# First batch's attention with four buffers of each kind, held loads, and a second warming product

## The chip, the cores and the metric

The program runs on one core of a Trainium2 chip. The metric is device time in microseconds (us), the median of several runs. PE is the matmul engine, ACT and DVE the two engines that work on vectors, POOL a fourth, slower one, and SP the engine that only issues DMAs.

## The reference

Multi-scale attention over 4 batches, 8 heads, 576 positions and 64 dimensions, then two feed-forward layers on 2304 tokens of width 512, all in float32:

```python
q_d, k_d, v_d = means over groups of 4 positions      # 144 pooled positions
out_up = np.repeat(sm_attn(q_d, k_d, v_d), 4, axis=2)
mask = np.abs(pos[:, None] - pos[None, :]) < 4        # a band of 7 positions
out_local = softmax(where(mask, q @ k.T / 8, -1e9)) @ v
x = (out_up + out_local) as (2304, 512)
x = (sigmoid(x @ w_gate) * (x @ w_val)) @ w_out       # d_ff 1536, "layer 1"
h = x @ w_in                                          # d_ff 2048, "layer 2"
out = (h * sigmoid(1.702 * h)) @ w_out2
```

## The kernel before

**Matmuls.** A float32 product is three PE products of reduced precision: `passes` (L939 to L941) multiplies hi x hi, hi x lo, lo x hi, where `parts_of` (L876, L879) has split each operand (`whi`, `wlo`, `xhi`, `xlo`, `ghi`, `glo`): ACT rounds the high part, DVE or POOL subtracts. Layer 1 is worked through by `visit`, batch by batch: for each of 12 hidden blocks `f`, `hidden` makes gate (part 0) and value (part 1) in a `ph` bank, four groups of three products each, and one block later `result` adds part 2 into four `acc` banks. Weights of layer 1 come from memory as 64-bit words, 512 KB for each part, and `convert` makes 32-bit ones: two passes on ACT (L865, L867) and one on DVE (L869). Four staging buffers `w64` take the loads; the 36 converted parts stay in the "weight places" `wr` and `w` for the later batches.

**Attention.** A `Job` is one batch `b` and one pair of heads `hp`, four for a batch. In order: `load` (qT, kT), `pools` (means over 4 on POOL, L638 and L640), `scores` (96 small matmuls, L674), softmax on DVE and ACT, `down` (pooled scores, L724, and `pooled_softmax`), `down_t` (transposes, L784), `values` (bands of v, L799, pooled values, L821, `up`, the sum `xf`, then `xhi` and `xlo`). v is pooled by PE with a matrix `ones` for batch 0 (`pool_tiles`, L592). The buffers of a kind are two (`sc` and `pdt` one), so a pair waits for an earlier one; only q and k of batch 0 have four, two of them in weight places not yet used (`qt0`, `kt0`). Batches 1 to 3 are "merged": pooled scores are made with the scores, half of the bands with the transposes; batch 1 also has its mask added by PE instead of DVE (L668, `masked`). Batch b's attention runs beside layer 1 of batch b - 1; batch 0's runs alone.

**What sets the order.** Every instruction is an `op` with an engine, an estimate of its time, the buffers it reads and writes, a due time and an earliest time. `Plan.order` walks a model of the five engines and always takes the ready `op` with the earliest due time; this fixes each engine's queue when the program is built, and on the chip each engine only follows its queue and waits for the others. Due times come from `T0` (layer 1 begins), `EARLY`, `FIRST`, `Job.t0` and `Job.t1`. Where PE's model has a gap, `order` fills it with "warming" products of zeros (L1433), at least one before each `op` other than the large products; they stop at the first product into `acc`. All DMAs are issued by SP, in the order of its queue.

Of the kernel before, what the change touches and what calls it, by code (L numbers as in the profile page):

```python
# [79 lines left out]
class Plan:  # L80
# [14 lines left out]
    WARM_LEAST = 1  # L95
    BEGIN = {"pe": 0.0, "act": 2000.0, "dve": 2200.0, "pool": 3900.0, "sp": 600.0}
# [47 lines left out]
    def order(self):  # L144
# [34 lines left out]
        while count:  # L179
# [109 lines left out]
def tile_multiscale_attention_gated_ffn(  # L289
# [83 lines left out]
    wslots = [Slot(x[:, i]) for x in low + top for i in range(2)]  # L373
    for f in range(NF1):
        for part in range(3):
            plan.ring(f"w{f}_{part}", [wslots[2 * NF1 + f if part == 2 else 2 * f + part]])
# [9 lines left out]
    first = [x.rearrange("p a b -> p (a b)").bitcast(F32) for x in top[-4:]]  # L386
    firsts = [Slot(x[:, :n]) for x, n in zip(first, (S + 8, KPAD + S + 5) * 2)]
    plan.ring("qt0", firsts[::2])
    plan.ring("kt0", firsts[1::2])
    for n, x in enumerate(wslots[-8:]):  # L390
        x.under = (firsts[n // 2],)
# [8 lines left out]
    qslots, kslots, vslots, pslots = (plan.rings[nm][0] for nm in ("qt", "kt", "vt", "pt"))  # L400
# [70 lines left out]
    for s in [*qslots, *plan.rings["qt0"][0]]:  # L471
        nc.vector.memset(s.t[:, S:], 0.0)
    for s in [*kslots, *plan.rings["kt0"][0]]:
        nc.vector.memset(s.t[:, :KPAD], 0.0)
        nc.vector.memset(s.t[:, KPAD + S:], 0.0)
# [44 lines left out]
    EARLY = 16.0e3  # L520
    AHEAD = 15.0e3
    FIRST = ((-14.0e3, 14.0e3), (-13.0e3, 16.0e3), (-12.0e3, 18.0e3))
# [19 lines left out]
    class Values:  # L542
# [6 lines left out]
        def load(self):  # L549
            b, c = self.b, slice(self.c0, self.c0 + VC)  # L550
            if b:
                self.vt, self.vd, self.vg = buf("vt"), buf("vd"), buf("vg")

            hp = self.job.hp
            d, after = (self.job.t0 - 3000.0, self.job.t0 - 12000.0) if b else (4500.0 * hp, 4500.0 * hp)
            for kh in range(2) if b else ():
                dma(self.vg.t[:, kh], v[b, kh * 4 * GH:(kh + 1) * 4 * GH, c].rearrange("(g r) d -> g r d", r=4),
                    GH * 4 * VC * 4, [], [(self.vg, kh)], d, after)
            d, after = (self.job.due(0.2), self.job.t0 - 9000.0) if b else (4000.0 * hp, 4000.0 * hp)
            if not b:  # L560

                if hp:
                    return
                c, n, t, d, after = slice(0, DM), 2, vboth.rearrange("p g h c -> p g (h c)"), -19.2e3, 3.5e3
                bs = [self.vt, halves[0, 1].vt]
            else:
                n, t, bs = 1, self.vt.t, [self.vt]
            for i in (0, 2, 1, 3):
# [5 lines left out]
                dma(t[32 * i:32 * i + 32, g0:g1], src, 32 * (g1 - g0) * n * VC * 4, [], [(x, i) for x in bs],  # L574
                    d, after)
            dma(t[3:NU + 1, 0], v[b, :NU - 2, c], (NU - 2) * n * VC * 4, [], [(x, 4) for x in bs], d, after)
            row = NQ * (NT - 1) - 3
            dma(t[96:96 + S - row, NG - 1], v[b, row:S, c], (S - row) * n * VC * 4, [], [(x, 5) for x in bs],
                d, after)

        def pool_tiles(self):
# [3 lines left out]
            at = self.job.due(0.55)  # L585
# [22 lines left out]
    class Job:  # L608


        def __init__(self, b, hp):
            self.b, self.hp = b, hp
            if b == 0:
                a, z = -EARLY, T0 - EARLY
            else:
                a, z = visits[b - 1]["t"] - LEAD, visits[b]["t"] - (SLACK if b < B - 1 else SLACK7)
            step = (z - a) / NHP
            self.t0, self.t1 = a + hp * step, a + (hp + 1.6) * step
            self.banks = twos if b == 0 else twos[:1]
            self.merged = b > 0 and (b, hp) != (1, 0)  # L620
# [3 lines left out]

        def load(self):
            b, hp = self.b, self.hp
            early = b == 0 and hp > 1
            self.qt, self.kt = (buf("qt0"), buf("kt0")) if early else (buf("qt"), buf("kt"))
            d, after = self.t0 - 4000.0, self.t0 - 13000.0
            if b == 0:  # L630
                d, after = -20.0e3 + 500.0 * hp, (0.0, 0.0, 9.5e3, 12.0e3)[hp]
            dma(self.qt.t[:, :S], qT[b, hp], P * S * 4, [], [self.qt], d, after)
            dma(self.kt.t[:, KPAD:KPAD + S], kT[b, hp], P * S * 4, [], [self.kt], d, after)

        def pool4(self, dst, src, bsrc, due):
            half = buf("half")
# [13 lines left out]
        def pools(self):  # L650
            for nm in ("qd", "kd", "sc", "nm", "sm", "pd", "nmd", "smd", "pt", "tt"):
                setattr(self, nm, buf(nm))
# [5 lines left out]
        def scores(self):  # L658
# [5 lines left out]
            masked = self.b == 1  # L664
# [15 lines left out]
            if not self.merged:  # L680
                op("pe", 1500.0 + 200.0 * masked, scored, [qt, kt, *[identb][:masked]], [ss, sc], when)
# [56 lines left out]
        def pooled_softmax(self, ss, c, at, masked):  # L738

            nmd, smd, pd = self.nmd, self.smd, self.pd  # L740
            op("dve", dve_ns(4 * G), lambda: nc.vector.reduce_max(
                nmd.t.rearrange("p (h r) -> p h r", h=2),
                ss.t[:GH, :, c:c + 2 * G].rearrange("p h (r k) -> p h r k", k=G), axis=AX.X),
               [ss, *masked], [nmd], at)
            op("act", 200.0, lambda: nc.scalar.mul(nmd.t, nmd.t, -SCALE_D), [], [nmd], at)
# [10 lines left out]
            def inv():  # L756
                nc.vector.tensor_scalar_add(smd.t, smd.t, 1.0e-9)
                nc.vector.reciprocal(smd.t, smd.t)

            op("dve", 305.0, inv, [], [smd], at)  # L760
# [8 lines left out]
        def down_t(self):  # L769
            self.pdt = buf("pdt")  # L770
# [32 lines left out]
        def values(self):  # L803
# [21 lines left out]
            xf = buf("xf")  # L825
# [28 lines left out]

    def convert(src, out, due, at=None, after=None):

        w = buf("w64")
        if at is None:
            at, after = due - 5000.0, due - AHEAD
        op("sp", P * 4096, lambda: nc.sync.dma_start(out=w.t, in_=src), [], [w], at, after)  # L860

        def words(n, dtype=I32):
# [3 lines left out]
            out.t.bitcast(F32), words(1, F32), AF.Prelu, scale=2.0 ** -112, alpha=-2.0 ** 32), [w], [out], due)  # L866
        op("act", act_ns(DM), lambda: nc.scalar.activation(  # L867
# [88 lines left out]
    def hidden(vi, f, t):  # L956
# [3 lines left out]
        xh, xl = xs[layer, j]  # L960
        hb = []
        th = buf("th")
        for part in range(2 if layer == 1 else 1):
            h = bank(hs_) if layer == 1 else fixed(f % 4)
            w = weights(vi, f, part, t)
            for k in range(NK):
# [3 lines left out]
                   w[0] + [(b, k) for b in (xh, xl)], [h] if part else [h, th], t))  # L970
# [407 lines left out]
    def make_ones():  # L1378
        nc.gpsimd.memset(ones.t, 0.0)
        for i in range(4):  # L1380
            c = 30 + 36 * (i % 2)
            part = ones.t[32 * i:32 * i + 32, c:c + 6]
            nc.gpsimd.memset(part, 1.0)
            nc.gpsimd.affine_select(out=part, in_=part, pattern=[[-4, 6]], compare_op=ALU.is_ge,
                                    fill=0.0, base=-3, channel_multiplier=1)
            nc.gpsimd.affine_select(out=part, in_=part, pattern=[[4, 6]], compare_op=ALU.is_ge,
                                    fill=0.0, base=6, channel_multiplier=-1)

    op("pool", 1500.0, make_ones, [], [ones], -4.0e3)
# [9 lines left out]
    halves[0, 0].load()  # L1399
# [79 lines left out]
```

## Time and profile before

| | us |
|---|---|
| runs | 922.09, 919.75, 920.48 |
| median | 920.48 |
| profiled execution | 919.47 |
| its span | 917.8 |
| PE busy | 907.8 (99%) |
| DVE, ACT, POOL busy | 691.3, 544.0, 80.5 |
| chain that ended last | 98% PE |

The span goes from the first to the last instruction of the profiled execution. A busy PE says little by itself, since warming products count too and the ends of pipelined matmuls are modelled: what a stretch is worth is read from the start times of its matmuls. Everything of attention of batch 0 lies in the first 61 us.

### The profile page before, as it was taken

To read this page: it belongs to the slowest core of one execution; us is meant where nothing else is said; L and a number is where in the kernel's file an instruction comes from. 1 tells how busy PE (TensorE), PEld (TensorE's weight loads), DVE (VectorE), ACT (ScalarE), POOL (GpSimd) and SP (SyncE) were. 2 spreads that over 40 slices of the span, in tenths; PEclk is the share of its full clock that TensorE was granted. 3 is DMA by queue.
4 is the path that set the end of the run, shared out by engine and by line. 5 is a ranking of instruction groups with operands and counts; after the bars stand their busy time and mean duration, and the time that the engine had idled before them with its cause. 6 is when DMAs were issued, how large, how long until landed. Compare 5 with 4: busy or idle time off the path is not lost.

```text
span 917.8 us, 18930 instructions
## 1 busy us (share of the span) xinstructions
PE 907.8 (99%) x7392; PEld 761.9 (83%) x7392; DVE 691.3 (75%) x1291; ACT 544.0 (59%) x1163; POOL 80.5 (9%) x124
## 2 busy tenths in 40 slices
PE   8999999999999999999999999999999999999998
PEld 4678888888888887889999998888888988888886
DVE  4777776776576766799999898878976779877742
ACT  4788885656666666665545655545665655535541
POOL 6221100111011100010000000000301001000000
PEclk9999999999999999999999999999999999999999
DMA  9559672574365734434311751002531002000431
GB/s 286 139 193 261 197 216 57 164 213 148 126 190 181 237 116 145 153 109 141 108 51 41 223 196 46 37 33 73 193 125 70 1 1 69 35 35 35 167 98 47
DMA packets 63949, 113.76 MB, mean 124 GB/s; under 512 B 8241, under 2 KB 29563, under 8 KB 63858
## 3 DMA queue, kind: packets, MB, share of 16 engines
q1 hardware_dynamic: 63858, 112.54, 38.7%
q8 instruction: 58, 0.95, 0.4%
q14 instruction: 33, 0.27, 0.1%
HBM read 82.37 MB, written 30.15 MB: 123 GB/s over the span
## 4 chain that ended last, share of the span: by engine, by line
PE 98%; POOL 1%; issue 0%; DVE 0%; POOLq 0%
PE ph L939 14%; PE ph L940 13%; PE ph L941 13%; PE acc L939 9%; PE acc L941 8%; PE acc L940 8%; PE pa L940 7%; PE pa L939 7%; PE pa L941 7%; PE pa L799 2%; PE pa L674 1%; PE pa L724 1%; PE acc L1433 1%; PE pa L821 1%; PE pa L784 1%; PE acc L799 1%
## 5 line engine op out<-in xcount | busy, mean ns | idle before, releaser
L939 PE MATMUL ph<-xhi,whi 128*128 128x512 f32 (+1 forms) x344 | 135.1, 393 | 0.0
L940 PE MATMUL ph<-xhi,wlo 128*128 128x512 f32 (+1 forms) x344 | 131.6, 383 | 0.0
L941 PE MATMUL ph<-xlo,whi 128*128 128x512 f32 (+1 forms) x344 | 131.5, 382 | 0.0
L876 ACT CAST whi<-w 128x512 fp32r<-128x512 f32 x140 | 85.5, 612 | 59.9 <-PE ph L941 33.2
L879 DVE TENSOR_TENSOR wlo<-w,whi 128x512 fp32r<-128x512 f32 x137 | 95.4, 698 | 29.7 <-ACT whi L876 29.3
L879 DVE TENSOR_TENSOR wlo<-wr,whi 128x512 fp32r<-128x512 f32 x106 | 69.8, 660 | 41.2 <-ACT whi L876 39.9
L939 PEld LDWEIGHTS ph<-xhi,whi 128*128 128x128 f32 x344 | 64.7, 188 | 15.2 <-issue 2.1
L941 PEld LDWEIGHTS ph<-xlo,whi 128*128 128x128 f32 x344 | 64.8, 188 | 12.9
L876 ACT CAST whi<-wr 128x512 fp32r<-128x512 f32 x106 | 60.2, 570 | 25.2 <-PE acc L941 12.2
L940 PEld LDWEIGHTS ph<-xhi,wlo 128*128 128x128 f32 x344 | 64.9, 189 | 11.7
L939 PE MATMUL acc<-ghi,whi 128*128 128x512 f32 (+1 forms) x192 | 73.7, 384 | 0.0
L941 PE MATMUL acc<-glo,whi 128*128 128x512 f32 (+1 forms) x192 | 72.3, 377 | 0.5 <-DVE glo L879 0.5
L1053 DVE TENSOR_TENSOR w<-pa,w 128x512 f32<-128x512 f32 (+1 forms) x112 | 70.4, 629 | 2.4 <-PE pa L941 1.9
L940 PE MATMUL acc<-ghi,wlo 128*128 128x512 f32 (+1 forms) x192 | 72.2, 376 | 0.0
L876 ACT CAST w<-w 128x512 fp32r<-128x512 f32 x62 | 37.9, 619 | 43.1 <-PE acc L940 23.6
L940 PE MATMUL pa<-w,wlo 128*128 128x512 f32 (+1 forms) x166 | 60.6, 365 | 0.0
L941 PE MATMUL pa<-w,whi 128*128 128x512 f32 (+1 forms) x166 | 60.6, 365 | 0.0
L939 PE MATMUL pa<-w,whi 128*128 128x512 f32 (+1 forms) x166 | 60.6, 365 | 0.0
L879 DVE TENSOR_TENSOR w<-w,w 128x512 fp32r<-128x512 f32 x58 | 41.2, 716 | 19.0 <-ACT w L876 18.9
L973 ACT ACTIVATE th<-ph 128x512 f32<-128x512 f32 (+1 forms) x44 | 24.6, 559 | 39.2 <-PE ph L941 39.0
L978 DVE SCALAR_TENSOR_TENSOR th<-th,ph 128x512 f32<-128x512 f32 (+1 forms) x44 | 28.1, 638 | 24.5 <-PE ph L941 19.6
L867 ACT ACTIVATE w<-w 128x512 int32<-128x512 uint32 x68 | 45.2, 670 | 0.0
(281 smaller groups left out, 2222.5 us busy)
## 6 DMA issues: line engine op xcount, KB each, us to landing
w<-w SPq DMA_DIRECT2D x68, 512.0 KB
w2d<-we SPq DMA_DIRECT2D x32, 256.0 KB
w<-gd SPq DMA_DIRECT2D x32, 256.0 KB
gd<-w SPq DMA_DIRECT2D x30, 256.0 KB
st<-x2d SPq DMA_DIRECT2D x52, 128.0 KB
w<-w2d SPq DMA_DIRECT2D x16, 256.0 KB
wr<-w2d SPq DMA_DIRECT2D x16, 256.0 KB
qt<-qT SPq DMA_DIRECT2D x14, 288.0 KB
```

The source lines that it names most:

```text
L674: nc.tensor.matmul(ss.t[32 * i:32 * i + 32, h, g * NU:(g + 1) * NU], qt.t[hs, NQ * t:NQ * t + 32], kt.t[hs, NQ * t:NQ * t + NU], start=not ...
L724: nc.tensor.matmul(ss.t[:GH, h, c + r * G:c + (r + 1) * G], qd.t[h * D:(h + 1) * D, r * GH:(r + 1) * GH], kd.t[h * D:(h + 1) * D, :], star ...
L799: nc.tensor.matmul(ss.t[h * D:(h + 1) * D, s, q:q + NQ], vt.t[ks, g, v0 + h * D:v0 + (h + 1) * D], tt.t[ks, h, g, :NQ], start=True, stop=T ...
L867: op("act", act_ns(DM), lambda: nc.scalar.activation(words(0), words(0, U32), AF.Copy, scale=2.0 ** -29 * (1.0 - 2.0 ** -12), bias=2.0 ** ...
L876: op("act", act_ns(n), lambda: nc.scalar.copy(vh(), vm()), [rm], [rh], due)
L879: return lambda: on.tensor_sub(vl(), vm(), vh().bitcast(F32))
L939: nc.tensor.matmul(o, lhi, rhi, start=first, stop=False, skip_group_check=more)
L940: nc.tensor.matmul(o, llo, rhi, start=False, stop=False, skip_group_check=more)
L941: nc.tensor.matmul(o, lhi, rlo, start=False, stop=last, skip_group_check=more)
L973: op("act", act_ns(n, True), lambda h=h: nc.scalar.activation(th.t[:, :n], h.t[:, :n], AF.Tanh, scale=0.5 if layer == 1 else 1.702 / 4.0), ...
L978: op("dve", dve_ns(n), lambda: nc.vector.scalar_tensor_tensor(th.t[:, :n], th.t[:, :n], 1.0, hb[-1].t[:, :n], op0=ALU.add, op1=ALU.mult), ...
L1053: op("dve", dve_ns(N), lambda: nc.vector.tensor_add(tmp.t[:, o, :N], b.t[:, :N], tmp.t[:, i, :N]), [b, (tmp, i)], [(tmp, o)], t)
```

## The change

For batch 0, attention gets more room: places of weights that are not needed yet hold two further `qt`, `kt`, `pt`, `tt`, `xf`, three further `sc` and up to three of `pd`, `pdt` and the small ones, and the order in which weights take the places is changed so that these are taken last. All pairs of batch 0 but the first become merged, and all have the mask from PE. The loads of q, k and v of batch 0 go through `dma_in_turn`: each one waits on SP until all older ones have landed but the last 0.9 MB; v goes ahead of the fourth pair instead of the third. No other DMA is planned before 17 us. Layer 1 is planned from 30 us instead of 37 (`T0`), the pairs of batch 0 start 3 us apart. For some pairs of batch 0 the means over 4, the scaling of the pooled weights and other steps move between POOL, ACT and DVE; `ones` is made on DVE. Of every three conversions one does the shift on DVE instead of ACT. From 25 us of the plan on at least two warming products stand before each small `op`, not one.

```diff
+    WARM_MORE = 25.0e3
-                                n = max(n, self.WARM_LEAST)
+                                n = max(n, self.WARM_LEAST + (t >= self.WARM_MORE))
...
+    over = [*low[-3:], *top[-6:]]
+    for n, x in enumerate(over):
+        if n < 3:
+            a, b_, c = parts_in(x, NS, 4 * G, 8 * NG)
+            some = [("sc", Slot(tiled(a))), ("pdt" if n == 2 else "pd", Slot(squares(b_)))]
...
+        elif n < 5:
+            some = [("xf", Slot(parts_in(x, S)[0]))]
+        else:
+            a, b_ = parts_in(x, NQK, NP)
+            some = [(("qt", "kt")[n % 2], Slot(a)), (("tt", "pt")[n % 2], Slot(tiled(b_)))]
...
+    for nm, some in early.items():
+        plan.ring(nm + "0", plan.rings[nm][0] + some)
...
-        op("sp", nbytes, lambda: nc.sync.dma_start(out=out_, in_=in_), reads, writes, due, after)
+        op("sp", nbytes, lambda: nc.sync.dma_start(out=out_, in_=in_), reads, writes, due, max(after, FREE))
+    FREE = 17.0e3
+    DEEP = 900.0e3
+    def dma_in_turn(out_, in_, nbytes, writes):
...
+        while behind and ahead + started[behind - 1][0] <= DEEP:
+            behind -= 1
+            ahead += started[behind][0]
+        def fn():
+            x = nc.sync.dma_start(out=out_, in_=in_).ins
+            started[n].append(x)
+            if behind:
+                tc.add_manual_dep(x, started[behind - 1][2].name, mybir.DependencyInfo(
+                    mybir.DependencyClass.Sync, mybir.DependencyReason.DATA), reason="loads in turn")
...
-    T0 = 37.0e3
+    T0 = 30.0e3
...
+    VAT = 3
+    VPOOL = (0,)
...
-            self.merged = b > 0 and (b, hp) != (1, 0)
+            self.merged = (b, hp) not in ((0, 0), (1, 0))
...
-            masked = self.b == 1
+            masked = self.b <= 1
...
+            if self.b == 0 and self.hp in VPOOL:
+                op("dve", dve_ns(S), lambda: nc.vector.reduce_sum(
+                    dst.t, src.rearrange("p (g r) -> p g r", r=4), axis=AX.X), [bsrc], [dst], due)
+                return
...
+        if nconv[0] % 3 == 2 and nconv[0] < 3 * NF1:
+            op("dve", dve_ns(DM, True), lambda: nc.vector.tensor_scalar(
+                out.t, out.t, 3, None, op0=ALU.logical_shift_left), [], [out], due, port=True)
...
-    op("pool", 1500.0, make_ones, [], [ones], -4.0e3)
+    op("dve", 700.0, make_ones, [ident], [ones], -20.0e3)
...
-    for x in jobs[:NHP]:
-        x.load()
...
+    for x in range(NHP):
+        if x == VAT:
+            halves[0, 0].load()
+        jobs[x].load()
```

What this does to the queues is seen at three places. On SP, at the start of the program, before (`qt`, `kt` and the weight places `w_117` to `w_120` take q and k of the four pairs, `vt` takes v, `w_86` is a staging buffer of weights):

```order
L511 DMA kt_124<-kT 128x576
L511 DMA vt<-v 32x5x512
L511 DMA vt<-v 32x6x512 x2
L511 DMA vt<-v 32x5x512
L511 DMA vt<-v 28x512
L511 DMA vt<-v 27x512
L511 DMA w_117<-qT 128x576
L511 DMA w_118<-kT 128x576
L511 DMA w_119<-qT 128x576
L511 DMA w_120<-kT 128x576
L860 DMA w_86<-w 128x512 x4
```

and now:

```order
L566 DMA kt_124<-kT 128x576
L566 DMA w_118<-qT 128x576
L566 DMA w_117<-kT 128x576
L566 DMA vt<-v 32x5x512
L566 DMA vt<-v 32x6x512 x2
L566 DMA vt<-v 32x5x512
L566 DMA vt<-v 28x512
L566 DMA vt<-v 27x512
L566 DMA w_120<-qT 128x576
L566 DMA w_119<-kT 128x576
L550 DMA w_86<-w 128x512 x3
```

q and k of the third pair (head pair 2) have moved ahead of v.

On PE, at the scores of head pair 2, before (`pa_159`, `acc_154`, `acc_155` are double banks, `warm` a warming product):

```order
L784 MATMUL pa_159<-ident,pd_139 72x72 x8
L1433 LDWEIGHTS warm
L1433 MATMUL acc_155<-warm 128x512
L799 MATMUL acc_154<-tt_128,vt 64x24 x24
L1433 LDWEIGHTS warm
L1433 MATMUL acc_155<-warm 128x512
L674 MATMUL acc_155<-w_118,w_117 32x30 x48
```

and now:

```order
L744 MATMUL pa_159<-mask,identb 128x180
L750 MATMUL pa_159<-w_117,w_118 32x30 x48
L801 MATMUL pa_159<-kd_134,qd_132 72x144 x4
L1542 LDWEIGHTS warm
L1542 MATMUL acc_154<-warm 128x512
L1542 LDWEIGHTS warm
L1542 MATMUL acc_154<-warm 128x128
L1542 LDWEIGHTS warm
L1542 MATMUL acc_154<-warm 128x128
L886 MATMUL acc_154<-ident,pd_138 72x72 x8
```

The scores of head pair 2 followed the bands of pair 0; now they stand, with the mask and their pooled scores, ahead of the transposes of pair 0 and of the pooling of v.

On PE, where layer 1 begins, before (`ph_149` is the bank of gate):

```order
L724 MATMUL pa_159<-kd_135,qd_133 72x144 x4
L939 MATMUL ph_149<-xhi_89,whi_78 128x512
L940 MATMUL ph_149<-xhi_89,wlo_82 128x512
L941 MATMUL ph_149<-xlo_91,whi_78 128x512
L1433 LDWEIGHTS warm
L1433 MATMUL acc_155<-warm 128x512
L1433 LDWEIGHTS warm
L1433 MATMUL acc_155<-warm 128x128
```

and now:

```order
L901 MATMUL acc_154<-w_120,vt 64x24 x24
L923 MATMUL acc_154<-wr_110,vd_137 64x144 x4
L1050 MATMUL ph_149<-xhi_89,whi_78 128x512
L1051 MATMUL ph_149<-xhi_89,wlo_82 128x512
L1052 MATMUL ph_149<-xlo_91,whi_78 128x512
L1050 MATMUL ph_149<-xhi_89,whi_78 128x512
L1051 MATMUL ph_149<-xhi_89,wlo_82 128x512
L1052 MATMUL ph_149<-xlo_91,whi_78 128x512
```

The first groups of layer 1 stood between blocks of attention of batch 0; now they follow the last block of it, and each other.

## Rows read from the trace of the kernel before

**Rows 1.** Stretch: us; busy PE, PEld, DVE, ACT, POOL (instructions); clock, DMA share, GB/s.

```profile
61.00:917.80 856.80, 852.17 (x6264) 725.61 (x6263) 649.56 (x1198) 503.63 (x1052) 54.63 (x66) 1.00 0.37 117
```

**Rows 2.** What PE waited for: us in total, times, longest.

```profile
PE pa L724 <- POOL kd L640: 3.3, 1, 3.3
...
PE acc L941 <- DVE glo L879: 0.5, 1, 0.5
```

**Rows 3.** Timeline of PE, layer 1: start us, duration us, engine, line, what.

```profile
36.55 0.79 PE L939 MATMUL ph<-xhi,whi 128*128 128x512 f32 x1
...
57.53 0.39 PE L939 MATMUL ph<-xhi,whi 128*128 128x512 f32 x1
...
60.26 0.39 PE L939 MATMUL ph<-xhi,whi 128*128 128x512 f32 x1
...
60.98 0.58 PE L939 MATMUL acc<-ghi,whi 128*128 128x512 f32 x1
```

**Rows 4.** Timeline of PE, blocks of attention of batch 0.

```profile
16.66 2.95 PE L592 MATMUL acc<-vt,ones 64*72 64x256 f32 x24
19.54 0.39 PE L1433 MATMUL acc<-warm 128*128 128x512 bf16 x1
19.77 0.67 PE L784 MATMUL acc<-ident,pd 72*72 72x72 f32 x8
20.27 0.38 PE L1433 MATMUL ph<-warm 128*128 128x512 bf16 x1
20.58 2.81 PE L592 MATMUL pa<-vt,ones 64*72 64x256 f32 x24
23.33 0.39 PE L1433 MATMUL acc<-warm 128*128 128x512 bf16 x1
23.65 0.89 PE L799 MATMUL acc<-tt,vt 30*64 30x24 f32 x48
24.47 0.71 PE L821 MATMUL acc<-pdt,vd 72*64 72x144 f32 x8
...
27.30 1.02 PE L674 MATMUL acc<-w,w 64*32 64x30 f32 x96
...
30.36 0.71 PE L724 MATMUL acc<-kd,qd 64*72 64x144 f32 x8
...
43.32 0.32 PE L668 MATMUL pa<-mask,identb 128*128 128x180 bf16 x2
```

**Rows 5.** Timeline of SP's DMA issues.

```profile
7.42 0.35 SPq L511 DMA_DIRECT2D w<-kT  x1
8.87 0.33 SPq L511 DMA_DIRECT2D w<-qT  x1
...
13.82 0.33 SPq L860 DMA_DIRECT2D w<-w  x1
```

**Rows 6.** Timeline of POOL, first use of q.

```profile
4.60 0.67 POOL L638 TENSOR_TENSOR half<-qt 128x288 f32<-128x288 f32 x1
```

**Rows 7.** Timelines of ACT and DVE, the steps behind the bands.

```profile
25.23 0.29 ACT L828 ACTIVATE up<-acc 128x144 f32<-128x144 f32 x1 [0.63 <-PE acc L821]
...
27.11 0.76 DVE L834 TENSOR_TENSOR xf<-acc,up 128x576 f32<-128x576 f32 x1 [0.31 <-PE acc L799]
...
27.91 0.62 ACT L845 CAST xhi<-xf 128x512 fp32r<-128x512 f32 x1
...
53.33 0.68 DVE L847 TENSOR_TENSOR xlo<-xf,xhi 128x512 fp32r<-128x512 f32 x1
```

**Rows 8.** Granted clock of PE by stretch, columns as in rows 1.

```profile
23.60:32.00 8.40, 8.40 (x315) 6.33 (x315) 5.51 (x9) 6.59 (x13) 2.63 (x3) 1.00 0.42 124
34.00:37.40 3.40, 3.40 (x103) 2.44 (x77) 2.70 (x7) 1.86 (x6) 2.28 (x3) 0.51 1.04 229
```

**Rows 9.** Timeline of PE, pooled scores in the stretch of 34 to 37.

```profile
35.38 1.24 PE L724 MATMUL pa<-kd,qd 64*72 64x144 f32 x8
```

**Rows 10.** Groups of ACT's instructions from 0 to 61 us: busy us, mean ns.

```profile
L867 ACT ACTIVATE w<-w 128x512 int32<-128x512 uint32 x9 | 6.0, 674 | 0.0
```

More of the change, by code (lines that the diff above doesn't have):

```diff
@@ L384, in tile_multiscale_attention_gated_ffn, with parts_in, tiled, squares @@
         aslots += ring(nm, n, shape, F32, apool)
[L386 to L391, printed above, removed]
+    def parts_in(x, *sizes):
+        flat, at, out_ = x.rearrange("p a b -> p (a b)").bitcast(F32), 0, []
+        for n in sizes:
+            out_.append(flat[:, at:at + n])
+            at += n
+        return out_
+    def tiled(x):
+        return x.rearrange("p (h g c) -> p h g c", h=2, g=NG)
+    def squares(x):
+        return x[:GH].rearrange("p (h r q) -> p h r q", h=2, r=2)
+    NS, NP, NQK = 2 * NG * NU, 2 * NG * 32, S + 8
+    early = collections.defaultdict(list)
+    over = [*low[-3:], *top[-6:]]
[3 more added lines that the diff above has]
+            some = [("sc", Slot(tiled(a))), ("pdt" if n == 2 else "pd", Slot(squares(b_)))]
+            if n < 2:
+                for i, nm in enumerate(("nm", "sm", "nmd", "smd")):
+                    y = c[:, i * 2 * NG:(i + 1) * 2 * NG].rearrange("p (h g) -> p h g", h=2) if i < 2 else \
+                        c[:GH, 4 * NG + 4 * (i - 2):4 * NG + 4 * (i - 1)]
+                    some.append((nm, Slot(y)))
+        elif n < 5:
[3 more added lines that the diff above has]
+            some = [(("qt", "kt")[n % 2], Slot(a)), (("tt", "pt")[n % 2], Slot(tiled(b_)))]
+        for nm, slot in some:
+            early[nm].append(slot)
+        for w_ in wslots:
+            if w_.tile.tensor is x.tensor:
+                w_.under = tuple(slot for _, slot in some)
     small = apool.tile([P, 4, 2, NG], F32, name="small", tag="small")
@@ L567, in load @@
                 n, t, bs = 1, self.vt.t, [self.vt]
+            into = (lambda *a: dma(*a[:3], [], a[3], d, after)) if b else dma_in_turn
             for i in (0, 2, 1, 3):
@@ L744, in pooled_softmax, with spread @@
                [ss, *masked], [nmd], at)
+            if self.b == 0 and self.hp not in APOOL:
+                flat = pd.t.rearrange("p h r q -> p (h r) q")
+                both, each = [(pd, 0), (pd, 1)], [(smd, 0), (smd, 1)]
+                def spread(x):
+                    return x.t[:, :, None].to_broadcast([GH, 4, G])
+                op("dve", dve_ns(4 * G), lambda: nc.vector.tensor_sub(
+                    pd.t, ss.t[:GH, :, c:c + 2 * G].rearrange("p h (r k) -> p h r k", k=G),
+                    spread(nmd).rearrange("p (h r) q -> p h r q", h=2)), [ss, nmd], both, at)
+                op("act", act_ns(4 * G), lambda: nc.scalar.activation(flat, flat, AF.Exp, scale=SCALE_D),
+                   [], both, at)
+                op("dve", dve_ns(4 * G), lambda: nc.vector.reduce_sum(smd.t, flat, axis=AX.X), both, each, at)
+                op("dve", 305.0, inv, [], [smd], at)
+                op("dve", dve_ns(4 * G), lambda: nc.vector.tensor_mul(flat, flat, spread(smd)), [smd], both, at,
+                   port=True)
+                return
             op("act", 200.0, lambda: nc.scalar.mul(nmd.t, nmd.t, -SCALE_D), [], [nmd], at)
@@ L960, in hidden @@
         xh, xl = xs[layer, j]
+        sooner = SOONER if (layer, j, f) == (1, 0, 0) else 0.0
         hb = []
@@ L964, in hidden @@
             h = bank(hs_) if layer == 1 else fixed(f % 4)
-            w = weights(vi, f, part, t)
+            w = weights(vi, f, part, t - sooner)
             for k in range(NK):
@@ L969, in hidden @@
                     k == 0, k == NK - 1),
-                   w[0] + [(b, k) for b in (xh, xl)], [h] if part else [h, th], t))
+                   w[0] + [(b, k) for b in (xh, xl)], [h] if part else [h, th], t - sooner))
                 t += q * vi["slow"]
@@ L1378, in make_ones @@
     def make_ones():
-        nc.gpsimd.memset(ones.t, 0.0)
+        nc.vector.memset(ones.t, 0.0)
         for i in range(4):
[L1381 to L1387, printed above, removed]
-    op("pool", 1500.0, make_ones, [], [ones], -4.0e3)
+            c, x = 30 + 36 * (i % 2), slice(32 * i, 32 * i + 32)
+            nc.vector.reduce_sum(ones.t[x, c:c + 6], ident.t[x, 32 * i + 3:32 * i + 27].rearrange(
+                "p (j r) -> p j r", r=4), axis=AX.X)
+    op("dve", 700.0, make_ones, [ident], [ones], -20.0e3)
     op("act", act_ns(P), lambda: nc.scalar.copy(identb.t, ident.t), [ident], [identb], 0.0)
```

87 lines of the change are left out of this document (58 added, 29 removed).

## The prediction

> **What bounds the kernel now.** I read the share of busy time by stretch first, then the waits of PE, then PE's timeline at the start, and only then the other engines. The reader is to see four things.
>
> From 61 us to the end the granted clock is 1.00 and PE is busy for 852 of 857 us [rows 1]; of PE's waits the trace shows one there, 0.5 us long [rows 2]. So behind 61 us the kernel is a fixed amount of matmul work, and nothing that the change does to DVE, ACT or the DMA queue can win time there; it can only lose it.
>
> Before 61 us it is not. The first matmul of the gated layer starts at 36.55 us, the first product that accumulates into `acc` at 60.98 us [rows 3]. I use the latter as the mark, X = 60.98. Sixteen groups of three products stand before it (48 matmuls); twelve matmuls in a row take 60.26 - 57.53 = 2.73 us, 0.2275 each [rows 3], so the 48 are worth 10.9 us, and the rest of the 24.4 us between 36.55 and X is attention of the first batch, and warming products, between the groups. Both kernels have the same 48 before the mark. In the order of the changed kernel, the rows behind the mark are those of before except for one: the pooled scores of batch 1's first head pair (8 matmuls) move from before the mark to behind it, 0.71 - 0.07 = 0.64 us (duration of such a block, less the 0.07 by which a block's end overlaps the next: 23.65 + 0.89 against 24.47) [rows 4]. So
>
> time after = 919.47 - (60.98 - X after) + 0.64 + whatever is newly waited for behind X.
>
> 919.47 us is the profiled execution's own time (span 917.8, 1.67 around it); the median of the three runs is 1.01 us above it, which I add at the end.
>
> **The change part by part.** *Loads.* Each DMA on SP waits until the DMA eight places earlier has landed, so issue times tell landings: the fourth load (kt of head pair 1) has landed at 7.42, the four large pieces of v by 8.87 to 13.82 [rows 5]. The four pieces are 1.442 MB in 6.40 us, 225 GB/s. In the change q and k of head pair 2 (2 x 0.295 MB) go ahead of v, 2.6 us at that rate: the last large piece lands at 13.82 + 2.62 = 16.4, and the two small ones behind it (0.11 MB, 0.5 us) at 16.9. The hold keeps up to 0.9 MB under way, 4.0 us of transfer. The first load is in use 4.60 us after the span began [rows 6], 1.3 us of that for its own bytes, so the delay from issue to landing is at most 3.3 us, under 4.0, and I cost the hold at nothing; without that cover see the second rival. Below: q and k move faster than v, and v is there at about 15.
>
> *Attention's buffers.* With four of each kind, scores of head pair 2 need no earlier pair to finish, and go ahead of the pooling of v; before, they follow it and two bands. What PE still has to do when v has landed is then, in the new order, with durations taken start to start [rows 4]:
> - pooling of v 2.88 + 2.75, two warming products at 0.29 (mean of 0.23, 0.31, 0.32): 6.21
> - head pair 3: mask 0.25, scores 1.02 - 0.07 = 0.95, pooled scores 0.64, one warming product 0.29: 2.13
> - 8 blocks of bands at 0.82: 6.56; 3 blocks of transposes at 0.50: 1.50; 4 blocks of pooled values at 0.64: 2.56
> - 7 pairs of warming products at 0.29 + 0.23 = 0.52: 3.64
>
> 22.6 us, so the gated layer starts at 16.9 + 22.6 = 39.5, later than before, but then it runs together: 48 x 0.2275 = 10.9, mask and scores of batch 1 1.2, two pairs of warming products 1.04. X = 39.5 + 13.2 = 52.7.
>
> This holds only if DVE and ACT keep ahead. The last is the fourth head pair: its pooled values end on PE at 39.5 + 0.07; then `up` 0.29, combine 0.76, `xhi` 0.62, `xlo` 0.68 [rows 7] make 41.9, and PE reaches the first product that reads it after six groups, at 39.5 + 6 x 0.683 = 43.6. Cover 1.7 us; every microsecond beyond it is one of X.
>
> *The rest.* The mask added by PE costs four blocks of 0.25, of which the first three lie where PE waits for v, and takes four adds off DVE. Pooling by 4 of head pair 0, and `ones`, go from POOL to DVE, so POOL starts on pair 1 earlier. A third of the weight conversions lose one ACT pass (0.67) and gain a DVE pass of an unseen form: no less than nothing and no more than ACT's 0.67 [rows 10], taken as half of that; behind the mark DVE is busy for 650 and ACT for 504 of 857 us [rows 1], so it costs nothing there. The second warming product is in the sum above: 9 extra at 0.23 make 2.1 us of X.
>
> *The clock.* [...] At half clock the pooled scores took 1.24 [rows 9] instead of 0.71 [rows 4]. I allow for one such stretch of 3.4 us: between nothing and half of it, 1.7; I take 1.0.
> [...]
>
> Sum: X = 52.7 + 1.0 = 53.7; 919.47 - 7.3 + 0.64 = 912.8; with 1.01 for the median **913.8**, say 913.5.
>
> **The rivals.**
> 1. *The clock falls through the attention stretch.* [...] Against: 8.4 us of the same mixture at 1.00 [rows 8]. Price: 16.4 us of the stretch are not pooling of v; at the ratio of pooled scores (1.17 against 0.64) they would grow by 13.6 us at most; half of that, 6.8, gives 52.7 + 6.8 = 59.5 and 919.6: no change that can be told.
> 2. *The hold starves the DMA queue.* For: SP issues in order, so a held load holds everything behind it, weights too. Against: 3.3 us of delay under 4.0 us of bytes. Price: if each of the six held DMAs up to the last piece of v loses 1 us, v lands at 22.9, X is 59.7: 919.8. The loads land in issue order before too, so in itself the hold may do nothing; then the sum stands.
> 3. *Slower: PE starves for weights behind X.* Before, nine conversions have had their second ACT pass by 61 us [rows 10]; in the new order only six stand on DVE ahead of the first `glo`. Behind X PE uses one part in 12 x 0.2275 = 2.73 us, and a part that starts from its load needs up to 3.3 us (as the first load above) and five passes on ACT and DVE in turn at about 0.67 [rows 10], 3.4: 6.7 us. If twelve parts in a row each come 1 us late, the 7.3 us won at X are gone and the kernel is at 926. It decides once the lead is used up, within two or three hidden blocks behind X. Against: the passes of different parts overlap, and ACT's three of a part take 2.0 us of the 2.73.
>
> **How the numbers follow.** Forecast 0.70, with its own range 909 (v at 15, clock never falls: X = 50.8, 910.9, less scatter) to 917.5 (cover of 1.7 us lost, two slow stretches). Rival 1 0.12, rival 2 0.08, rival 3 0.10. A change under 0.3%, 2.8 us, can't be told from none here: 917.7 to 923.2 is "same". Faster: nearly all of the forecast, a third of rivals 1 and 2: 0.74. Slower: most of rival 3: 0.08. Same: 0.18. The range 908 to 920 takes in the forecast and most of rivals 1 and 2, a little over 0.8.
>
> **What would show it.** First accumulating product at 52 to 55 us; first matmul of the gated layer at 38 to 41 and no attention block of batch 0 after it; the 3.3 us that PE waits for POOL's pooled k of pair 1 [rows 2] gone; last piece of v landed by 16 to 18 (start of the v pooling). Rival 1 would show as a granted clock near 0.5 between 17 and 39; rival 2 as DMA share well under 1 between 5 and 16 and a late v pooling; rival 3 as waits of PE for `wlo` or `whi` behind the mark. I am wrong if PE waits for `xlo` or `xf` for more than a few microseconds, or if waits stand behind the mark where before had 0.5 us.

## The result and the profile after

The changed kernel takes 926.45 us (median of four runs, 924.27 to 927.91) against 920.2 for the kernel before: the ratio of the means is 1.0062, with a 95% interval of 1.0037 to 1.0087. It is slower, by 0.6%; the forecast was 913.5 and faster. The profile below is of the fastest of the four, 924.27; its mean clock is 0.987, that of the other three 0.982 to 0.984. In several experiments below the executions of one program fall into two groups, told apart by the granted clock; their times are then given as two groups.

Behind the mark nothing went wrong. The stretch that answers to [rows 1], same columns:

```profile
61.00:922.00 861.00, 856.25 (x6286) 728.11 (x6284) 658.85 (x1222) 502.91 (x1058) 52.28 (x63) 1.00 0.38 118
```

The clock is 1.00 and PE is busy as before. What PE waited for there, and below it the four longest waits of PE up to 66 us (us in total, times, longest), against [rows 2]:

```profile
PE acc L1052 <- DVE glo L990: 0.4, 1, 0.4
```

```profile
PE acc L801 <- issue: 1.6, 1, 1.6
PE acc L901 <- issue: 1.6, 1, 1.6
PE acc L1542 <- DVE warm L509: 1.0, 1, 1.0
PE acc L801 <- DVE kd L709: 0.3, 1, 0.3
```

The 3.3 us for POOL's pooled k are gone, as predicted, and no weight is late behind the mark. There are two stops of 1.6 us that name no engine and no DMA ("issue"); the kernel before has one such stop, of 1.0 us. The marks themselves, on the timeline of PE, against [rows 3]: the pooling of v, the bands in which the second stop lies, two blocks behind it, the first layer-1 product and the first one into `acc`.

```profile
17.46 0.87 PE L662 MATMUL acc<-vt,ones 64*72 64x256 f32 x6
...
27.55 0.76 PE L901 MATMUL acc<-tt,vt 30*64 30x24 f32 x35
29.86 0.42 PE L901 MATMUL acc<-tt,vt 30*64 30x24 f32 x13 [1.56 <-issue]
...
31.39 1.13 PE L901 MATMUL acc<-tt,vt 30*64 30x24 f32 x48
32.45 1.23 PE L923 MATMUL acc<-wr,vd 72*64 72x144 f32 x8
33.61 1.03 PE L1542 MATMUL ph<-warm 128*128 128x512 bf16 x2
34.58 1.49 PE L901 MATMUL pa<-w,vt 30*64 30x24 f32 x48
36.00 1.17 PE L886 MATMUL pa<-ident,wr 72*72 72x72 f32 x8
...
49.85 0.80 PE L1050 MATMUL ph<-xhi,whi 128*128 128x512 f32 x1
...
64.08 0.58 PE L1050 MATMUL acc<-ghi,whi 128*128 128x512 f32 x1
```

The pooling of v starts at 17.46 (forecast: 16.9, when v has landed), and up to 27.55 everything is in its place. Layer 1 starts at 49.85 (39.5), and the mark stands at 64.08 (53.7), later than before's 60.98. In between a block of bands takes 1.42 us from start to start (34.58 to 36.00) where [rows 4] show 0.82. The granted clock by stretch, against [rows 8], columns as in [rows 1], says why:

```profile
11.40:14.80 3.40, 3.35 (x107) 2.15 (x107) 1.90 (x5) 0.88 (x5) 0.00 (x0) 0.50 0.86 184
16.00:30.00 14.00, 12.28 (x273) 8.21 (x274) 10.38 (x26) 10.28 (x31) 4.51 (x8) 1.00 0.84 264
30.00:32.00 2.00, 2.00 (x60) 1.34 (x61) 1.32 (x4) 1.03 (x3) 0.00 (x0) 0.97 0.58 221
32.00:52.00 20.00, 20.00 (x315) 13.96 (x312) 7.32 (x12) 8.68 (x18) 4.45 (x3) 0.50 0.39 115
52.00:54.00 2.00, 2.00 (x9) 1.60 (x9) 2.00 (x4) 1.03 (x2) 0.00 (x0) 0.91 1.04 382
```

There are two falls. The first, of 3.4 us, lies behind the first stop and ahead of the pooling of v. The second lasts from 32 to 52 us: the granted clock is 0.50, PE is busy for all of the 20 us, and the clock comes back when layer-1 products follow one another (the first at 49.85; 0.91 from 52 to 54). DVE is busy for 7.3 and ACT for 8.7 of these 20 us: ACT waits 9.1 us for PE, DVE 4.3 for PE and 9.1 for ACT. The clock is the bound of this stretch.

### The profile page after: what moved, and what is told of

The parts are those of the page before. It is cut to its first block, busy times and chain, and to the rows that moved or that the text cites. A ratio compares the mean times of both kernels' runs of the same rounds, so it can differ in the third digit from the quotient of the medians.

```text
span 922.5 us, 18877 instructions
## 1 busy us (share of the span) xinstructions
PE 912.6 (99%) x7385; PEld 766.1 (83%) x7385; DVE 696.3 (75%) x1317; ACT 533.3 (58%) x1135; POOL 71.7 (8%) x104
## 4 chain that ended last, share of the span: by engine, by line
PE 98%; DVE 1%; issue 1%; ACT 0%; DVEq 0%
PE ph L1050 14%; PE ph L1051 13%; PE ph L1052 13%; PE acc L1050 9%; PE acc L1052 8%; PE acc L1051 8%; PE pa L1050 7%; PE pa L1051 7%; PE pa L1052 7%; PE pa L901 2%; PE pa L750 1%; PE pa L923 1%; PE pa L886 1%; PE pa L801 1%; PE acc L901 1%; PE acc L662 1%
## 5 line engine op out<-in xcount | busy, mean ns | idle before, releaser
L990 DVE TENSOR_TENSOR wlo<-wr,whi 128x512 fp32r<-128x512 f32 x106 | 67.6, 639 | 36.5 <-ACT whi L987 35.4
L987 ACT CAST whi<-wr 128x512 fp32r<-128x512 f32 x106 | 60.0, 569 | 26.4 <-PE acc L1052 12.6
L1051 PE MATMUL pa<-w,wlo 128*128 128x512 f32 (+1 forms) x166 | 60.6, 365 | 0.0
L1050 PEld LDWEIGHTS acc<-ghi,whi 128*128 128x128 f32 x192 | 36.0, 188 | 7.4 <-issue 1.7
```

Of the source, the lines that this page charges most:

```text
L987: op("act", act_ns(n), lambda: nc.scalar.copy(vh(), vm()), [rm], [rh], due)
L990: return lambda: on.tensor_sub(vl(), vm(), vh().bitcast(F32))
L1050: nc.tensor.matmul(o, lhi, rhi, start=first, stop=False, skip_group_check=more)
L1051: nc.tensor.matmul(o, llo, rhi, start=False, stop=False, skip_group_check=more)
```

## The experiments

All but one change the changed kernel. Where only the number of warming products changes, the loop that issues the ordered instructions counts them, and a table says how often the n-th is issued (once where it is not named):

```diff
     for o in plan.order():
-        o.fn()
+        n = 1
+        if not hasattr(o, "eng"):
+            n = TIMES.get(warmed, 1)
+            warmed += 1
+        for _ in range(n):
+            o.fn()
```

Number 30 stands at 25.35 us of the changed kernel, ahead of the bands and transposes that come before the second stop. 31 to 44 are the seven pairs that follow: the first pair (27.02 us) stands right ahead of the bands with the stop, the other six behind it. "A block" below means after each of the seven.

**Is it the stop?** `TIMES = {30: 9}`:

> The changed kernel with eight more warming products in one place, between the pooled scores of the last head pair of batch 0's first half and what follows them (25.4 us in the trace of the changed kernel), so that TensorE takes 8 x 0.21 = 1.7 us longer to come to the place where it stood still for 1.56 us (28.30 to 29.86 us) with no wait named, and its instructions can be there. Theory 1 (the standing still starts the fall of the clock, and the small blocks then can't bring it back): the stop shrinks below 0.3 us, the clock is 1.00 from 30 to 50 us, the first layer-1 product comes at about 42, the first product into acc at about 55 to 56, and the time is about 917 us. Theory 2 (the mixture of small blocks with warming products is too thin in itself): the clock falls to half in this stretch all the same, first acc product at 63 to 65, time 925 to 927. Theory 3 (the held loads bring weights or code late): nothing changes, the stop stays at its length.

Measured: 925.14 (922.5 to 926.42, six executions). The stop is gone, and the clock falls all the same, at 34.4 us. Stretches of this execution:

```profile
24.00:34.00 10.00, 10.00 (x300) 6.71 (x289) 7.00 (x15) 5.84 (x12) 1.68 (x4) 1.00 0.43 122
36.00:50.00 14.00, 14.00 (x220) 10.03 (x216) 6.53 (x10) 6.16 (x13) 4.45 (x3) 0.50 0.49 160
```

PE is busy for all of the 10 us ahead of the fall. Theory 1 falls as the only cause: the bands, transposes and pooled values with two products between can lose the clock without any stop.

**What do fewer or more products do behind a fall?** `TIMES = {32: 0, 34: 0, ..., 44: 0}` (one a block) and `{31: 2, 32: 2, ..., 44: 2}` (four a block):

> The changed kernel with one warming product in place of two after each of seven blocks of batch 0's attention (from the transposes of pair 1 on). The stop of 1.6 us stands before them and stays in all theories. Theory 1 and 2 alike: the clock is at half behind it with one product as with two, so seven products of 0.49 us (half clock) go, 3.4 us: first acc product at 60.6 instead of 64.08, time about 922.5. If the second product does hold the clock up somewhere, the half-clock stretch is longer than 31.9 to 52.2 less 3.4 us, and the gain smaller than 1.5 us.

> The changed kernel with four warming products in place of two after each of seven blocks of batch 0's attention. Theory 1 with a mixture of two products just too thin to bring the clock back: with four it comes back within some 5 us of the stop at 28.3 us, the stretch 31 to 50 us takes about 11 + 14 x 0.22 = 14 us and not 18.5, first acc product at 59 to 61, time 920 to 922. Theory 2, in the form that the blocks themselves keep it down whatever stands between them: 14 products of 0.49 us are added, first acc product at 71, time about 933.

One a block: 924.2 (922.79 to 925.0); in the profiled execution the stop was 4.3 us and the mark stood at 64.8 where 60.6 was expected, so the stop ate the saving. Four a block: 929.55 to 933.45 in ten executions, with the clock at half for 29 us behind a stop of 1.8 us, and 918.12 in one whose mean clock was 0.997:

```profile
31.00:60.00 29.00, 29.00 (x368) 18.14 (x365) 8.45 (x14) 10.71 (x21) 4.46 (x3) 0.50 0.33 102
```

So four products between blocks did not bring the clock back in these 29 us; each of them only costs about twice its time (0.49 us against 0.23). The expected recovery within 5 us did not come.

**Is it the hold?** `DEEP = 900.0e6` in place of `900.0e3`:

> The changed kernel with no load held back for older ones (the limit on bytes on the way is set so high that it never holds). Theory 1 and 2: the stop at 28.3 us is for TensorE's instructions and not for a held load, the clock falls as before, first acc product at 62 to 66, time 924.5 to 928.5. Theory 3 (the hold makes the stop, by what it lets through at once later or by late loads): the stops at 9.9 and 28.3 us shrink, first acc product below 60, time below 922. The other way, if the hold helps: v lands after 17.5 us, the V pooling starts at 20 or later, and the time is 929 or more.

Measured: 918.5 to 919.1 in seven executions and 926.88 to 930.87 in five. Neither expectation was right. The first stop grew to 5.88 us, and the pooling of v came later than 20 us, as the last clause said, but not because v was late: PE names no wait for v, and comes to it late from its own stop:

```profile
16.32 0.88 PE L801 MATMUL acc<-kd,qd 64*72 64x144 f32 x5 [5.88 <-issue]
...
23.10 2.81 PE L662 MATMUL acc<-vt,ones 64*72 64x256 f32 x24
...
35.19 0.89 PE L901 MATMUL acc<-tt,vt 30*64 30x24 f32 x48
...
45.78 0.50 PE L1050 MATMUL ph<-xhi,whi 128*128 128x512 f32 x1
...
58.87 0.58 PE L1050 MATMUL acc<-ghi,whi 128*128 128x512 f32 x1
```

The pooling starts 5.6 us later than in the changed kernel, and yet seven executions are 7 us faster than its median. In the profiled one of them the clock holds through the same blocks in the same order:

```profile
24.00:58.00 34.00, 34.00 (x751) 24.66 (x748) 26.84 (x48) 24.04 (x53) 10.45 (x10) 1.00 0.53 159
```

This execution prices the clock. From the bands at 35.19 to the first layer-1 product it takes 10.59 us; the changed kernel takes 18.46 for the same rows (31.39 to 49.85): 7.9 us. From there to the mark it takes 13.09 against 14.23: 1.1 us.

**Must the stop go and the blocks be thicker?** Four kernels: three products a block with the filled stop (`{30: 9, 32: 2, 34: 2, ..., 44: 2}`); the hold put on the first 28 DMAs, weights too; this hold with three a block; this hold with three a block and the filled stop. The hold:

```diff
-        op("sp", nbytes, lambda: nc.sync.dma_start(out=out_, in_=in_), reads, writes, due, max(after, FREE))
+        def fn():
+            x = nc.sync.dma_start(out=out_, in_=in_).ins
+            if len(issued) < MOST:
+                held(x, nbytes)
...
+    MOST = 28
```

`held` makes the DMA wait until all older ones have landed but the last `DEEP` bytes (0.9 MB), as `dma_in_turn` does.

> The first experiment (eight more warming products ahead of the place of the stop, which made the stop vanish but not the fall of the clock, 34.4 us) with three warming products in place of two after each of the seven attention blocks behind it. Theory 2a (two products a block are just too few to hold the full clock, three hold it): clock 1.00 from 16 us on, first acc product at 56 to 57 (52.7 as forecast, 0.6 for v, 8 x 0.21 and 7 x 0.23 for the products), time about 917, 8 us under the first experiment's. Theory 2b (no number of such products holds it once the array has little else to do): the fall comes as before, first acc product at 66 to 67, time 927.

> The changed kernel with the hold (at most 0.9 MB of loads under way) put on the first 28 DMAs of SP, the first weights among them, and not on q, k and v alone; the order is the same on every engine. Theory 3a (the stop at 28 us is code that comes late behind the 3.7 MB of weights and q, k, v of batch 1 that SP issues between 15 and 20.4 us; without any hold the stop at 11 us was 5.9 us): the stop of 1.6 us shrinks below 0.8 us. The clock may still fall, since it did so without the stop in the first experiment: then time 923 to 926; if it holds, first acc product about 54, time 914 to 916. If the stop has nothing to do with loads under way, it stays 1.5 us or more.

> The hold on the first 28 DMAs and three warming products in place of two after each of the seven attention blocks. Theory 2a with 3a: no stop, clock 1.00 from 16 us on, first acc product at 55, time about 915, under both the kernel before (919.9) and the change (926.45). Theory 2b: half clock from about 32, 928. If the stop stays, the clock falls behind it, as with four products a block, and the time is 928 to 930.

> The changed kernel with the hold on the first 28 DMAs, eight more warming products ahead of the bands where TensorE stood still, and three products a block behind them. Theory 4 (the clock falls from either of two causes, a stop for code or a stretch of blocks with too little between, and both must go; behind a fall the small blocks never bring it back): in all executions the clock holds to 60 us, first acc product at 56 to 57, time 916 to 917, all within 1 us. If a third cause is there, some executions are at 926 to 930, as 8 of 12 of the kernel without the hold on the weights (fill_three) were.

- Filled stop and three a block: 916.36 to 916.93 in four executions with a mean clock of 0.997 to 1.00, 927.29 to 930.33 in eight with 0.984 to 0.986. The fast four are what theory 2a gave, to 0.7 us, the first product into `acc` at 56.51; the others are 2b's.
- Hold on all, nothing else: 923.06 (922.33 to 924.45). There is no second stop, and the clock falls at 27.7 us all the same: a second kernel that loses it without a stop.
- Hold and three a block: 928.05 (926.23 to 928.2), with a stop of 0.8 us in the bands.
- All three together: 915.17 to 918.04 in ten executions, 926.87 and 929.75 in two; median 916.39, a ratio of 0.9977 (0.9957 to 0.9997) to the kernel before.

The last beats both kernels, by little. Its clock in the stretch of attention, its first layer-1 product and its mark:

```profile
26.00:43.00 17.00, 17.00 (x466) 11.57 (x465) 10.70 (x20) 9.54 (x19) 6.39 (x6) 1.00 0.56 162
```

```profile
42.69 0.50 PE L1066 MATMUL ph<-xhi,whi 128*128 128x512 f32 x1
...
55.75 0.58 PE L1066 MATMUL acc<-ghi,whi 128*128 128x512 f32 x1
```

Filling the stop alone held the clock in none of six executions, the third product with the hold in none of five, filling and third product without the hold on the weights in four of twelve, all three in ten of twelve. The hold and the filling with two products a block were not run, so what the third product adds is not separated.

**How much is enough?** As the last, with four more products ahead of the bands in place of eight, and with four a block in place of three:

> As the run before it with four more products ahead of the bands in place of eight (0.9 us less). Theory 4: with the hold the code needs less time, the stop is under 0.3 us, first acc product at 55 to 56, time 915 to 916 in all executions. If the four products give the code too little time, a stop of 0.4 us or more is left and some executions fall to half clock: 926 to 929.

> The ninth experiment with four warming products a block in place of three. If the two executions of twelve of it that were at 926.9 and 929.8 fell because the blocks are still too thin, none falls here: all within 917.2 to 918.8 (seven products more, 7 x 0.22 = 1.6 us). If they fell by a stop for code, some 2 of 12 fall again: 929 to 931.

With four more: 914.56 to 917.41 in six executions, 925.46 to 929.11 in six; in the profile, of the first group, stops of 0.5 and 0.3 us are left in the bands, and the clock holds through them. The second group has no profile; that a longer stop made it fall is not shown. With four a block: 917.25 to 919.75 in eleven, 928.22 in one (median 917.9, ratio 0.9993, 0.9974 to 1.0012). One of twelve against two of twelve can't be told apart: the fourth product does not rule the fall out, that it makes it rarer is not shown, and its price is 1.5 us. What took the last execution was not seen.

**What brings the clock back?** `TIMES = {33: 15}`, one run of products in the half-clock stretch:

> The changed kernel with 14 more warming products in one run, behind the first pooled values of pair 1 (33 us, in the half-clock stretch). Theory: a run of products with nothing between brings the clock back, as the first layer-1 products did at 52, and blocks with two or four products between do not. The clock rises to 1.00 within the run (7 us at half clock at most, 36 to 40 us), and the blocks behind take 0.82 and 0.64 us again and not 1.42 and 1.16; first acc product at 60 to 62, time 922.5 to 924.5. If the clock falls again in the blocks behind the run, first acc product at 66 to 69, time 928 to 931.

Measured: 921.43 (919.57 to 922.52, nine executions), first product into `acc` at 61.2, within the expected 60 to 62; the time is 1 us below the range. Clock by stretch, and the timeline of the run (14 and the pair that stood there) and of what follows it:

```profile
30.00:36.00 6.00, 6.00 (x32) 2.69 (x29) 0.69 (x2) 1.36 (x3) 0.00 (x0) 0.50 0.09 34
37.00:50.00 13.00, 13.00 (x349) 9.31 (x348) 8.56 (x11) 8.09 (x16) 4.29 (x3) 1.00 0.45 124
```

```profile
31.50 6.13 PE L1542 MATMUL ph<-warm 128*128 128x512 bf16 x16
37.56 0.89 PE L901 MATMUL acc<-tt,vt 30*64 30x24 f32 x48
38.38 0.71 PE L923 MATMUL acc<-wr,vd 72*64 72x144 f32 x8
```

The run brings it back (0.50 up to 36 us, 1.00 from 37), and in this execution the blocks with two products between them then keep it; no other of the nine has a time or a mean clock (0.993 to 0.998) that leaves room for a second long fall. Fourteen products in one place save 5 us; the same fourteen spread over the blocks cost 5.

**Does the kernel before gain from it?** Its own stop of 1.01 us, with five more products ahead of it (numbers 30 and 31 of its order):

> The kernel before, with five more warming products ahead of its own stop of 1.01 us with no wait named (32.09 to 33.10 us): two behind the pooled values of pair 0 and three behind the pooled scores next to them, 5 x 0.227 = 1.1 us of work. Theory 4: the stop goes, the fall of the clock behind it (0.50 from 34.0 to 37.4) goes with it, and the blocks there take 0.95, 0.64 and 0.2275 us again: 1.08 - 0.95, 1.17 - 0.64 and some 0.8 us on the first three layer-1 products and warming products: about 1.4 us less, time 918 to 918.8 against 919.6. If the fall has nothing to do with the stop: no gain or 0.1 us, 919.5 or more.

Measured: 920.2 (919.02 to 925.48), ratio 1.0017 (1.0005 to 1.0029): no gain. The stop left its place and came back further on:

```profile
33.52 0.89 PE L799 MATMUL pa<-tt,vt 30*64 30x24 f32 x48
...
38.63 0.27 PE L1433 MATMUL acc<-warm 128*128 128x128 bf16 x2 [0.86 <-issue]
```

The time is that of the second case, the profile that of the first: the fall at 34 us went with the stop (the clock is 1.00 from 19.4 us on), but an earlier one, behind the wait for POOL, was longer in this execution (12.6 to 19.4), and the products and the new stop cost what was saved. Since the stop only moved, the run does not tell the cases apart. One thing it shows: the new stop lies among the first layer-1 products (from 36.58 us on), and the clock stays at 1.00 around it:

```profile
33.00:40.00 7.00, 6.14 (x170) 3.85 (x169) 5.95 (x14) 4.87 (x18) 2.54 (x4) 1.00 0.83 219
```

**Layer-1 products in place of warming ones.** The kernel with all three together, with the first two groups of layer 1 (and what they depend on) moved up, each in place of three warming products; the products 41 to 44 are left out:

```diff
+    MOVED = {41: 0, 43: 1}
...
+    first = [o for o in row if o in plan.large][:2]
...
+            if warmed in MOVED:
+                x = first[MOVED[warmed]]
...
+                x.fn()
```

> The ninth experiment (hold on the first 28 DMAs, eight more products ahead of the bands, three products a block) with useful work in place of six of the products: the first two groups of three layer-1 products, which read pair 0 and 1, stand where three warming products each stood, behind the last transposes and behind the pooled values next to them. Theory: layer-1 products between the attention blocks do the warming products' work, as in the kernel before; the clock holds as often, and 6 x 0.2275 us = 1.4 us go: first acc product at 54.4 for 55.75, 914 to 915.2 in the executions that hold, median under 915.5. If the fourth pair's xlo is now late (its lead shrinks from six groups to four), PE waits up to 1.4 us there and nothing is won: 916.4.

Measured: 918.58 (915.34 to 924.69), ratio 0.9994 (0.9975 to 1.0013): nothing won against the kernel before, and its median is 2.2 us above that of the kernel it was made from. In its profile the clock holds from 16.2 us on, but PE waits 0.65 us for POOL's `xlo` in the first moved group, and the first stop is 1.57 us: the wait was expected at the fourth pair and came at the first.

## Why the prediction was wrong

*The frame was right.* Time behind the mark is fixed: the moved block of pooled scores costs what was said (the 150th large product behind the mark comes 0.63 us later than in the kernel before; forecast 0.64). Span less mark is 858.4 here and 856.8 before, 1.6 against the 0.64 of the sum; of the other 1.0 us some 0.4 comes between the 1500th and the 2000th large product and some 0.6 behind the last; neither was traced to a line.

*Loads and buffers were right.* The DMA eight places behind the last large piece of v is issued at 16.49 us here and at 16.62 without the hold, so by the prediction's own reading that piece had landed by then in both (in the trace of before SP waits 1.1 us for the load of `kt` that stands eight places ahead of the DMA issued at 7.42):

```profile
16.49 0.86 SPq L550 DMA_DIRECT2D qt<-qT  x1
```

```profile
16.62 0.33 SPq L550 DMA_DIRECT2D qt<-qT  x1
```

The hold costs nothing, and rival 2 did not occur. That the pooling of v starts 0.6 us late here, and 5.6 us later still without the hold, is not the loads: PE comes out of its first stop at 11.45 and at 16.32, and the pooling follows 6.0 and 6.8 us behind. The sum had no such stop.

*The list of PE's work was right at full clock.* With four more products ahead of the bands and seven behind, at full clock, the mark stood at 54.95. Eleven products less at 0.227 make 52.45; the forecast without the clock was 52.7. That it is so close is in part luck: there the pooling of v starts at 15.30, 1.6 us before the 16.9, and 0.84 us of stops lie behind it. From the start of the pooling to the mark, less products and stops, it takes 36.3 us against the 35.8 of the sum. The cover of DVE and ACT held as well: PE did not wait for `xlo` or `xf`.

*The step that failed* is "The clock": "I allow for one such stretch of 3.4 us ... I take 1.0". The stretch was 20 us long. It measured 7.9 us in the blocks and 1.1 in the first products, and the second stop, that the sum did not have, 1.56; with 0.6 for the late start of the pooling that is 11.1 of the 11.4 us between 52.7 and 64.08. The 3.4 us are those of [rows 8], at a granted 0.51; the 1.0 taken from them was the author's estimate, and no run shows it. Rival 1 named what happened, with a chance of 0.12 and a price of 6.8, half of its own upper bound of 13.6; the clock cost 9.0.

Two readings led there. First, [rows 8] show 8.4 us of "the same mixture" at 1.00, but it was not the same: in that stretch before has the scores and pooled scores of head pair 2 ([rows 4]: 27.30 and 30.36) between the bands, which the change had moved ahead of the pooling of v. What was left is bands, transposes and pooled values. That this is why the stretch can't hold the clock is argued; that it can lose it without a stop is shown (the filled stop, and the hold on the first 28 DMAs alone). It is not the whole of it: without any hold the same blocks in the same order, with two products between and no stop among them, kept the clock in the profiled execution and by their times in six more of twelve, and with the hold on 28 DMAs they lost it in all five. Second, the half clock of 34.0 to 37.4 in [rows 8] was read as the length of such an event, and not together with what stood ahead of it, a stop of 1.01 us in the bands:

```profile
33.10 0.41 PE L799 MATMUL pa<-tt,vt 30*64 30x24 f32 x12 [1.01 <-issue]
```

The fall ended there beside the first layer-1 products (36.55 in [rows 3]), which before stood between the blocks of attention; the change gathered them behind the last block, and so, it seems, took away what ends a fall. That a run of full products ends it is shown (the run of sixteen products in 6.13 us, from 0.50 to 1.00, and here the layer-1 products from 49.85 on, from 0.50 to 0.91 in 52 to 54 us); that layer-1 products did so in the kernel before is read from its rows, not tried alone: the run that moved two groups back up did it in a kernel that mostly keeps its clock.

In the second fall, 20 us long, the rows show no pause of PE (20.00 of 20.00 us busy).

What stays open is why one execution keeps the clock and the next doesn't: the program and the order are the same (916.4 and 928.6 us of one kernel).

## What to carry over

Here the layer-1 products were gathered behind a stretch of small matmuls, and PE's granted clock in that stretch fell to 0.50 for 20 us (3.4 us in the kernel before). That the gathering took away what keeps or restores the clock is the author's reading. With such a change, price the whole stretch at the lower level (here a granted 0.50), and look for what would bring the clock back. Warming products spread behind a fall cost twice their time (0.49 us against 0.23) and did not bring the clock back (0.50 for 29 us with four a block); one uninterrupted run of them did (16 in 6.13 us). With the first 28 DMAs held and three products a block, eight more products placed ahead of the bands in which the stop lay kept the clock in ten of twelve executions, not in all. A stretch that can go either way has to be judged by several executions, with the clock of each.

## What the runs showed that was not expected

What the runs show points to PE standing still for its own code. The stops without a releaser come at the same count of instructions in both kernels, whatever stands there. Instructions on PE (matmuls and weight loads in brackets) before the two stops of the changed kernel, and before the 1.01-us stop of the kernel before:

```profile
0.00:11.40 11.40, 8.53 (x222) 4.57 (x223) 8.69 (x38) 3.84 (x12) 7.73 (x26) 1.00 0.80 244
11.40:29.80 18.40, 16.70 (x382) 10.97 (x381) 13.13 (x31) 11.75 (x37) 4.51 (x8) 0.91 0.85 249
```

```profile
0.00:33.05 33.05, 27.75 (x604) 16.46 (x605) 17.70 (x50) 17.37 (x50) 17.80 (x50) 0.95 0.80 240
```

445, 1208, and in the kernel before 1209. The second stop of the kernel without the hold (22.6 us), the later stop of the kernel with four more products ahead of the bands (33.0) and the moved stop of the kernel before (38.6) come at 700, 1464 and 1463:

```profile
0.00:22.58 22.58, 15.15 (x350) 8.59 (x350) 13.38 (x50) 6.86 (x25) 9.91 (x30) 0.85 0.95 275
```

```profile
0.00:33.00 33.00, 29.51 (x732) 18.80 (x732) 24.71 (x75) 18.37 (x55) 13.23 (x34) 1.00 0.80 236
```

```profile
0.00:38.60 38.60, 33.30 (x731) 19.64 (x732) 22.12 (x60) 19.85 (x59) 19.92 (x53) 0.91 0.78 231
```

In all fifteen profiles PE has 23 such stops, and each stands at one of these four counts. Just ahead of the second stop's end, between 27.0 and 28.6 us, the DMA queue that the profile calls "instruction" moves one piece (packets, MB, share):

```profile
q8 instruction: 1, 0.02, 5.3%
```

Over the whole span of the changed kernel it moves 58 pieces, 0.95 MB, 16 KB a piece. Each of the 23 stops ends 0.9 to 1.6 us behind the end of a piece (in the changed kernel pieces end at 10.00 and 28.51 us, and the stops at 11.45 and 29.86; in the kernel before 31.49 and 33.10), the stop at 445 behind the first piece that the trace records, those at 700, 1208 and 1464 behind the second, fourth and fifth. By that order the distances between the four counts, 255, 508 and 256 recorded instructions, are one, two and one piece: some 255 recorded instructions of PE a piece, an estimate from the counts. The stops also follow the loads: the first is 5.88 us without the hold, 1.0 to 1.6 with it on q, k and v, and with it on the weights too under 0.9 or none in five of six profiles (1.57 in the sixth). The second is 1.56 to 4.3 with the hold on q, k and v, and none or 0.8 with it on the weights too (in the kernels without more products at number 30). That PE waits for such a piece when it comes late is the author's reading: the counts, the pieces and two changes of the loads support it, but no run moved the code alone.
